# A sparse-attention, gated-MLP and token-mixing block on one core: v's tail between its pairs, the bias split in attention 0, merged x evictions, and batch 1's softmax with the main chain's priority

## The chip, the cores and the metric

The kernel runs on one core of one Trainium2 chip. The metric is the device time of one execution in microseconds (us). Runs are compared by their medians, and one execution of each kernel was recorded by the hardware profiler.

## The reference, cut to what matters

```
attn: q, k, v of 4 batches x 8 heads x 576 x 64
  heads 0-3: mask (0 <= i-j < 32);  heads 4-7: mask (i >= j and i%32 == j%32)
  x = softmax(mask(q k^T / 8)) v                    -> 4 x 576 x 512
h = relu(x @ w_in);  u, v = h[..., :512], h[..., 512:]
v_n = (v - mean(v)) / sqrt(var(v) + 1e-6)           over the 512 columns
x2 = (u * (w_spatial @ v_n + b_spatial)) @ w_out
theta = x2 @ w_theta
y = x2 + w_tok_r @ (x2 cos theta) + w_tok_i @ (x2 sin theta)
out = y + relu(y @ w_ch)
```

## The kernel before, in words

Every large product is made of float16 halves: an operand is split into a high and a low part, and three passes (high x high, low x high, high x low) go through TensorE. `PASS` is that list. The main chain of one batch is `main_v` (the v half of the first product, and its normalisation into `vn`), `main_mid` (u, the spatial product `sp`, the out product `x`, the theta product `th`) and `main_end` (the token product `y` and the channel product `c`). In `main_v` the 576 rows are two pairs of 128-row blocks (v0 and v1, one PSUM tile of two banks each) and a tail of 64 rows (v2). `v_relu` evicts a pair and takes the statistics of each block on VectorE; `norm` makes the reciprocal deviations of the blocks that it is given with `rstd`, 12 small VectorE operations on the tile `rs` whatever the number of columns, and `norm_q` then scales each block and splits it into high and low part.

Attention is a side chain. Batch 0's is `attention0`: nine groups of 64-row blocks in a software pipeline, s = 0 to 11, with scores, shift by the maximum (`gr_shift`, VectorE), exponential (`gr_exp`, ScalarE), transpose (`gr_turn`), product with v (`gr_pv`) and eviction into the two halves of `xT` (`gr_out`, which calls `gr_parts`). Within attention 0 each engine's instructions stay in the order in which the program gives them (the set `pinned`); the conversions of w_in are put between the steps by the table `aside`. After it, a list scheduler orders each engine's queue by priority and readiness. An operation called through `hv`, `ha` or `hg` has a priority 200 places ahead of its place in the program, and the main chain's vector and scalar operations use these; the attention of batches 1 and 2 (`attention1`, eight quads of blocks, with `qd_softmax` and `qd_div`) uses the plain priority. `others` puts the steps of attention and of the weight conversions (`conv`) between the main chain's matmuls by a count of matmul columns.

Three buffers of two PSUM banks (`pm`) serve the main chain's tiles and the attention's scores; two single banks (`sc` and `av`) serve attention's transposes and products. `gr_parts` evicts a PSUM bank in runs: blocks of one head that follow each other form a run, and each run costs one ScalarE and one VectorE operation, which take turns on the bank.

The bias of the spatial product, `b_sp`, stands with the tail of w_spatial in the tile `wspt`: row 64 holds its high part and row 96 its low part. `sp_tail` loads it on the SP queue into the staging buffer `x2f`, after the tail, and splits it there.

Of the kernel before, what the change touches and what calls it, by code (L numbers as in the profile page):

```python
# [19 lines left out]
ALU = mybir.AluOpType  # L20
# [12 lines left out]
AHEAD = 200  # L33
N32 = 3
LAG16 = 3
V_ORDER = (0, 1, 2)
E_WAY = 'aaaadaaadaa'
E_WHI = 'aaaa'
E_WLO = 'ggvv'
# [30 lines left out]
def kernel(  # L70
# [249 lines left out]
    def sp_tail():  # L320
        stg = pair(stage()[0].bitcast(F32), S)
        for j in range(2):
            nc.sync.dma_start(stg[j * TL:(j + 1) * TL, 0, :], w_spT[T0:S, :])
        nc.sync.dma_start(stg[TL:TL + 1, 1, :], b_sp)
        nc.sync.dma_start(stg[96:97, 1, :], b_sp)
        nc.scalar.activation(wspt[:, 0, :], stg[:, 0, :], AF.Copy, scale=SPS)
        nc.vector.scalar_tensor_tensor(wspt[0:TL, 1, :], stg[0:TL, 0, :], SPS, wspt[0:TL, 0, :],
                                       op0=ALU.mult, op1=ALU.subtract)
        nc.scalar.activation(wspt[TL:TL + 1, 1, :], stg[TL:TL + 1, 1, :], AF.Copy, scale=SPS)
        nc.scalar.activation(wspt[96:97, 1, :], stg[96:97, 1, :], AF.Copy, scale=SPS)  # L330
        nc.vector.scalar_tensor_tensor(wspt[96:97, 1, :], stg[96:97, 1, :], SPS, wspt[96:97, 1, :],
                                       op0=ALU.mult, op1=ALU.subtract)

    def tok_load(i, raw):
# [294 lines left out]
    def gr_parts(b, local, blocks, xt, by=1):  # L629

        xh = xT[b % 2]
        runs = []
        for i, (hp, blk) in enumerate(blocks):
            if runs and runs[-1][0] == hp and (local or blk < 10):
                runs[-1][3] += 1
            else:
                runs.append([hp, blk, i, 1])
        for hp, blk, i, n in runs:
            src = xt[:, QB * i:QB * (i + n)]
            if local:  # L640
                dst = [xh[:, e, hp, QB * blk:QB * (blk + n)] for e in range(2)]
            else:
                nr = min(3, STRIDE - 3 * blk)
                r0, o = (3 * (blk - blk % by), blk % by) if nr == 3 else (3 * blk, 0)
                dst = [xh[:, e, hp, :].rearrange("p (j r) -> p j r", r=STRIDE)
                       [:, :, r0:r0 + n * nr * (by if nr == 3 else 1)]
                       .rearrange("p j (n t r) -> p j n t r", n=n, r=nr)[:, :, :, o] for e in range(2)]
                src = src.rearrange("p (n c) -> p n c", c=QB)[:, :, 0:nr * NCLS].rearrange(
                    "p n (r j) -> p j n r", j=NCLS)
            nc.scalar.activation(dst[0], src, AF.Copy)  # L650
            nc.vector.tensor_tensor(dst[1], src, dst[0], ALU.subtract)

    def attention0(aside):

        xf = xT[1].rearrange("p e c n -> p (e c n)").bitcast(F32)
        vf = wtok.rearrange("p e i n -> p (e i n)").bitcast(F32)
        qk = kts + [xf[:, i * 2 * S:(i + 1) * 2 * S].rearrange("p (j n) -> p j n", j=2) for i in range(2)]
        q, k = [t[:, 0] for t in qk], [t[:, 1] for t in qk]  # L660
        v = [vf[:, i * 9 * VW:(i + 1) * 9 * VW].rearrange("p (n d) -> p n d", n=9) for i in range(2)]
        v23 = vf[:, 18 * VW:30 * VW].rearrange("p (h n d) -> p h n d", h=2, n=6)
        v += [v23[:, i] for i in range(2)]
        load_qk(0, 0, q[0], k[0], 0, 4 * QB)
        load_qk(0, 1, q[1], k[1], 0, S, nc.scalar)
        nc.scalar.activation(x2f[:, 0, 0:1], halfpi, AF.Exp)
        make_masks()
        load_qk(0, 0, q[0], k[0], 4 * QB, S)
        load_vl(0, 0, v[0])
        load_vl(0, 1, v[1])  # L670
        aside[-1][0]()
        load_qk(0, 2, q[2], k[2], 0, S)
        load_qk(0, 3, q[3], k[3], 0, S)
        aside[-1][1]()
        load_vs(0, v23)
        load_mask16()
        un = {}
        for s in range(NG + 3):
            mid, end = aside.get(s, ((), ()))
            if s < NG:  # L680
                if s % 4 == 3:
                    banks = pa("sc"), pa("av")
                else:
                    two = pm("at")
                    banks = two[:, 0, :], two[:, 1, :]
                t = s2("smx")
                sm, pT = t[:, 0, 0:384], t[:, 1, 0:512].rearrange("p (n k) -> p n k", n=4)
                st = att_p.tile([P, 2, 6], F32, tag="st", name="st", bufs=4)
                un[s] = banks, sm, pT, st
                gr_scores(s, q, k, banks[0])  # L690
                gr_shift(s, banks[0], sm, st)
            if s >= 3:
                banks, sm, pT, st = un.pop(s - 3)
                gr_out(0, s - 3, pT, banks[1])
            if 1 <= s <= NG:
                banks, sm, pT, st = un[s - 1]
                gr_turn(s - 1, sm, banks[1].rearrange("p (n k) -> p n k", n=4), pT)
            if s < NG:
                gr_exp(s, un[s][1])
            for f in mid:  # L700
                f()
            if 2 <= s < NG + 2:
                banks, sm, pT, st = un[s - 2]
                gr_pv(s - 2, v, pT, banks[0][:, 0:3 * VW].rearrange("p (i n) -> p i n", i=3), st, pT)
            for f in end:
                f()
# [42 lines left out]
        if not partial:  # L749
            masks()  # L750

    def qd_softmax(g, sc, sm, st):
        local, slots, ns, w = qd_size(g)
        n = 2 * ns
        sv = sc[:, :, 0:ns * w].rearrange("p j (n c) -> p j n c", c=w)
        mx = st[:, 0, 0:n].rearrange("p (j n) -> p j n", j=2)
        nc.vector.tensor_reduce(out=mx, in_=sv, op=ALU.max, axis=mybir.AxisListType.X)
        nc.vector.tensor_tensor(sm[:, 0:n * w].rearrange("p (j n c) -> p j n c", j=2, c=w), sv,
                                mx.unsqueeze(3).broadcast_to([P, 2, ns, w]), ALU.subtract)
        nc.scalar.activation(sm[:, 0:n * w], sm[:, 0:n * w], AF.Exp, scale=0.125)  # L760

    def qd_div(g, sm, st):

        local, slots, ns, w = qd_size(g)
        n = 2 * ns
        p, sums = sm[:, 0:n * w].rearrange("p (n c) -> p n c", c=w), st[:, 1, 0:n]
        nc.vector.tensor_reduce(out=sums, in_=p, op=ALU.add, axis=mybir.AxisListType.X)
        nc.vector.tensor_scalar(sums, sums, 1e-9, 1.0 / XS, op0=ALU.add, op1=ALU.mult)
        nc.vector.reciprocal(sums, sums)
        nc.vector.tensor_tensor(p, p, sums.unsqueeze(2).broadcast_to([P, n, w]), ALU.mult)  # L770

    def qd_places(g):

# [43 lines left out]
    def attention1(b):  # L817
# [20 lines left out]
        for s in range(NQ + 2):  # L838
            def turn():
                sm, pT, st = un[s - 1]  # L840
                qd_turn(s - 1, sm, pa4("av"), pT)

            if s == NQ:
                turn()
            if s >= 2:
                sm, pT, st = un.pop(s - 2)
                qd_px(b, s - 2, v, pT)
            if s < NQ:
                sm = att_p.tile([P, 512], F32, tag="sm", name="sm", bufs=2)
                pT = att_p.tile([P, 4, P], F32, tag="pT", name="pT32", bufs=2)  # L850
                st = att_p.tile([P, 2, 8], F32, tag="st", name="st", bufs=4)
                un[s] = (sm, pT, st)
                sc = pm("a1")
                qd_scores(s, q, k, sc)
                qd_softmax(s, sc, sm, st)
            if s in loads:
                f, hp = loads[s]
                f(hp)
            if 1 <= s < NQ:
                turn()  # L860
            if s < NQ:
                qd_div(s, *un[s][::2])
            yield


# [114 lines left out]
    def main_v(b):  # L980
# [43 lines left out]
        def v_mm(ps, i, c):  # L1024
            for n, (xe, we) in enumerate(PASS):
# [2 lines left out]
                    ps, xh[:, xe, c, i * P:(i + 1) * P], win[:, we, c, DM:2 * DM],  # L1028
                    start=(c == 0 and n == 0), stop=(c == NC - 1 and n == 2)).ins.name))

        if b == 0:
            ps = [pm("v0")]

# [11 lines left out]
            yield  # L1045
            some(1, (2,))
            yield
            for pr in range(2):
                some(pr, (3,))
                yield  # L1050
                v_relu(pr, ps[pr])
            norm((0, 1))
        for pr in V_ORDER if b else V_ORDER[2:]:
            ps = pm(f"v{pr}")
            if pr == 2:
                tail_mm(ps[:, 0, :], xh, win, slice(DM, 2 * DM))
                yield
            else:
                for t in range(2):
                    for c in range(NC):  # L1060
                        v_mm(ps[:, t, :], 2 * pr + t, c)
                    yield
            v_relu(pr, ps)
        norm((2,) if b == 0 else (0, 1, 2))

    def main_mid(b):
        xh = xT[b % 2]
# [332 lines left out]
```

## Time and profile before

| | us |
|---|---|
| median of 3 runs | 491.31 |
| the runs | 491.95, 491.31, 489.02 |
| the profiled execution | 488.88 |
| its span, first to last instruction | 487.0 |
| TensorE busy in the span | 467.9 |
| VectorE busy | 300.2 |
| ScalarE busy | 268.6 |
| GpSimd busy | 72.4 |

The span is what the trace covers; the 1.9 us between it and the execution's time lie outside of it. A matmul's busy time is modelled, so TensorE's share is read with the list of its waits beside it.

### The profile page before, as it was taken

What the parts mean: (1) busy time and instruction counts of PE and PEld (TensorE: products, weight loads), DVE (VectorE), ACT (ScalarE), POOL (GpSimd) and SP (SyncE); (2) the same over time, 40 slices, a digit from 0 to 9 for tenths busy, and PEclk for the clock granted to TensorE, in tenths of its full rate; (3) what the DMA queues carried; (4) which work ended last, traced back from release to release, by engine and by line L of the source; (5) the groups of instructions that cost most, each with busy time, mean ns of one, the idle gap of its engine ahead of it and who ended that gap; (6) DMA issues with size and microseconds to landing.
All of it is one profiled execution on the core that took longest, in us unless ns stands there. A gap on an engine that the chain in (4) does not pass through costs nothing. (4 is left out here: it accounts for less than half of the span.)

```text
span 487.0 us, 10793 instructions
## 1 busy us (share of the span) xinstructions
PE 467.9 (96%) x4440; PEld 351.5 (72%) x4440; DVE 300.2 (62%) x652; ACT 268.6 (55%) x480; POOL 72.4 (15%) x68
## 2 busy tenths in 40 slices
PE   6889998899999999999999999999999999999996
PEld 5665666677577778777568777777567777777775
DVE  3766997955998546752787878762686121227412
ACT  2668878788954334455945667754942022149202
POOL 2043025120015100201005110111005200210320
PEclk8999999999999999999999999999999999999999
DMA  6989446558860155100381345330450020003502
GB/s 177 288 260 286 187 138 217 171 182 243 158 153 1 63 168 147 54 1 2 85 216 53 88 125 159 66 44 1 68 127 2 1 98 0 1 2 74 122 0 99
DMA packets 71820, 52.72 MB, mean 108 GB/s; under 512 B 50584, under 2 KB 59992, under 8 KB 71770
## 3 DMA queue, kind: packets, MB, share of 16 engines
q1 hardware_dynamic: 71466, 51.42, 38.5%
q8 instruction: 35, 0.57, 0.5%
q10 hardware_dynamic: 304, 0.61, 0.4%
q14 instruction: 15, 0.12, 0.1%
HBM read 35.36 MB, written 4.72 MB: 82 GB/s over the span
## 5 line engine op out<-in xcount | busy, mean ns | idle before, releaser
L107 PE MATMUL y<-wtok,zf 128*128 128x288 f16 x864 | 107.2, 286 | 0.0
L107 PEld LDWEIGHTS <-zf 128*128 128x128 f16 x864 | 84.1, 98 | 22.2 <-issue 1.2
L107 PE MATMUL sp<-wsp,vn 128*128 128x288 f16 x384 | 50.7, 286 | 1.2 <-ACT u L107 1.2
L107 PE MATMUL x<-zf,wout 128*128 128x288 f16 x384 | 49.6, 287 | 0.0
L107 PE MATMUL v<-win,xT 128*128 128x512 f16 (+1 forms) x240 | 48.7, 380 | 0.9 <-DVE xT L107 0.6
L107 PE MATMUL u<-xT,win 128*128 128x288 f16 x384 | 49.2, 286 | 0.0
L107 PEld LDWEIGHTS <-vn 128*128 128x128 f16 x416 | 40.3, 98 | 11.4 <-issue 1.4
L107 PE MATMUL th<-x2h,wth 128*128 128x288 f16 x384 | 47.9, 286 | 0.0
L107 POOL TENSOR_TENSOR x2h<-x2f,x2h 128x576 f16<-128x576 f32 x19 | 26.2, 1382 | 142.4 <-issue 66.1
L107 PE MATMUL c<-x2h,wch 128*128 128x288 f16 x360 | 45.2, 286 | 0.0
L107 PEld LDWEIGHTS <-wth 128*128 128x128 f16 x384 | 37.6, 98 | 9.7 <-issue 0.2
L107 PEld LDWEIGHTS <-wch 128*128 128x128 f16 x384 | 37.4, 98 | 9.2
L107 PEld LDWEIGHTS <-win 128*128 128x128 f16 x384 | 37.4, 98 | 9.1
L107 PEld LDWEIGHTS <-wout 128*128 128x128 f16 x384 | 36.7, 98 | 9.5
L107 PEld LDWEIGHTS <-xT 128*128 128x128 f16 (+1 forms) x240 | 21.1, 100 | 24.9 <-issue 2.2
L107 ACT ACTIVATE x2h<-x2f 128x576 f16<-128x576 f32 (+1 forms) x28 | 20.9, 747 | 24.8 <-DVE x2f L107 23.5
L107 ACT ACTIVATE o<-c 128x576 f32<-128x576 f32 x15 | 9.7, 644 | 34.9 <-PE c L107 34.7
L107 DVE TENSOR_TENSOR ta<-ta,x2f 128x1152 f32<-128x1152 f32 (+1 forms) x17 | 21.7, 1284 | 11.2 <-ACT ta L107 11.2
L107 DVE SCALAR_TENSOR_TENSOR x2f<-y,x2f 128x576 f32<-128x576 f32 x16 | 12.0, 752 | 25.4 <-PE y L107 25.3
L107 POOL TENSOR_TENSOR zf<-u,zf 128x576 f16<-128x576 f32 x8 | 10.2, 1278 | 115.3 <-ACT zf L107 115.3
L107 DVE SCALAR_TENSOR_TENSOR o<-x2f,o 128x576 f32<-128x576 f32 (+1 forms) x17 | 12.2, 722 | 23.6 <-ACT o L107 23.6
L107 DVE TENSOR_TENSOR u<-u,sp 128x576 f32<-128x576 f32 x16 | 12.0, 750 | 22.2 <-PE sp L107 22.2
(144 smaller groups left out, 724.4 us busy)
## 6 DMA issues: line engine op xcount, KB each, us to landing
out_dram<-o SPq DMA_DIRECT2D x15, 288.0 KB
kt<-in_qp_dram SPq DMA_DIRECT2D x8, 288.0 KB
qs<-in_qd_dram SPq DMA_DIRECT2D x8, 288.0 KB
x2f<-in_w_in_dram SPq DMA_DIRECT2D x2, 1024.0 KB
zf<-in_w_in_dram SPq DMA_DIRECT2D x2, 1024.0 KB
xT<-in_w_ch_dram SPq DMA_DIRECT2D x2, 1024.0 KB
kt<-in_kzl_dram SPq DMA_DIRECT2D x8, 152.0 KB
ks<-in_kl_dram SPq DMA_DIRECT2D x4, 304.0 KB
```

The source lines that it names most:

```text
L107: ins = f(*args, **kwargs)
```

## The change

- **v's tail.** In batch 0 the tail's product and its eviction come after the first pair's last matmuls and before the second pair's, not after both. One `norm` over all five blocks takes the place of two (pairs, then tail). In the other batches the order stays.
- **Bias.** The two rows of the bias are loaded by two DMAs of GpSimd's queue into a tile of their own, behind the making of the masks, and split at the head of step s = 1 of attention 0: two ScalarE copies and a VectorE operation.
- **Merged evictions.** Where two neighbouring heads have the same single block in a bank, `gr_parts` evicts both in one run: one run fewer for the group that holds block 8 of heads 0 and 1, one fewer for the pair of last blocks in attention 0's group 6, and three fewer in the mixed quad of batches 1 and 2.
- **Priority.** `qd_softmax` and `qd_div` of batch 1 issue their VectorE operations through `hv`.

```diff
-        nc.sync.dma_start(stg[TL:TL + 1, 1, :], b_sp)
-        nc.sync.dma_start(stg[96:97, 1, :], b_sp)
...
-        nc.scalar.activation(wspt[TL:TL + 1, 1, :], stg[TL:TL + 1, 1, :], AF.Copy, scale=SPS)
-        nc.scalar.activation(wspt[96:97, 1, :], stg[96:97, 1, :], AF.Copy, scale=SPS)
-        nc.vector.scalar_tensor_tensor(wspt[96:97, 1, :], stg[96:97, 1, :], SPS, wspt[96:97, 1, :],
+
+    def bias_load():
+        t = s1("bias")
+        for r in (TL, 96):
+            nc.gpsimd.dma_start(t[r:r + 1, :], b_sp)
+        return t
+
+    def bias_part(t):
+        for r in (TL, 96):
+            nc.scalar.activation(wspt[r:r + 1, 1, :], t[r:r + 1, :], AF.Copy, scale=SPS)
+        nc.vector.scalar_tensor_tensor(wspt[96:97, 1, :], t[96:97, :], SPS, wspt[96:97, 1, :],
                                        op0=ALU.mult, op1=ALU.subtract)
...
-            if runs and runs[-1][0] == hp and (local or blk < 10):
+            if runs and runs[-1][0] == hp and runs[-1][4] == 1 and (local or blk < 10):
                 runs[-1][3] += 1
+            elif runs and runs[-1][0] == hp - 1 and runs[-1][1] == blk and runs[-1][3] == 1:
+                runs[-1][4] = 2
...
         make_masks()
+        bias = bias_load()
...
             mid, end = aside.get(s, ((), ()))
+            if s == 1:
+                bias_part(bias)
...
-    def qd_softmax(g, sc, sm, st):
+    def qd_softmax(b, g, sc, sm, st):
+        dv = hv if b == 1 else nc.vector
...
-        nc.vector.tensor_reduce(out=mx, in_=sv, op=ALU.max, axis=mybir.AxisListType.X)
+        dv.tensor_reduce(out=mx, in_=sv, op=ALU.max, axis=mybir.AxisListType.X)
...
-    def qd_div(g, sm, st):
+    def qd_div(b, g, sm, st):
+        dv = hv if b == 1 else nc.vector
...
+        def tail():
+            ps = pm("v2")
+            tail_mm(ps[:, 0, :], xh, win, slice(DM, 2 * DM))
+            yield
+            v_relu(2, ps)
...
+            some(0, (3,))
+            yield
+            v_relu(0, ps[0])
+            for _ in tail():
+                yield
+            some(1, (3,))
+            yield
+            v_relu(1, ps[1])
...
-        norm((2,) if b == 0 else (0, 1, 2))
+        norm((0, 1, 2))
```

## Rows read from the trace of the kernel before

**Rows 1.** What TensorE waited for, 31 to 106 us: total, times, longest.
```profile
PE av L107 <- DVE sm L107: 2.2, 4, 1.1
PE av L107 <- DVE xT L107: 1.7, 1, 1.7
PE sp L107 <- ACT u L107: 1.2, 1, 1.2
...
PE v L107 <- POOL win L107: 0.3, 1, 0.3
```
**Rows 2.** Busy time of each engine by stretch, granted clock, DMA share, GB/s.
```profile
48.47:61.51 13.04, 11.52 (x124) 8.69 (x123) 12.98 (x49) 10.82 (x17) 0.00 (x0) 1.00 0.51 189
61.51:89.64 28.13, 26.10 (x355) 19.48 (x355) 25.36 (x47) 22.01 (x33) 11.88 (x9) 1.00 0.55 180
89.64:107.69 18.05, 15.77 (x163) 11.78 (x161) 12.66 (x28) 14.27 (x25) 2.73 (x2) 1.00 0.59 192
...
119.62:487.00 367.38, 361.63 (x3220) 274.44 (x3217) 210.37 (x441) 181.58 (x346) 44.27 (x31) 1.00 0.30 74
```
**Rows 3.** TensorE in order of time: start, duration, instruction, idle before and releaser.
```profile
61.51 1.63 PE L107 MATMUL sp<-wsp,vn 128*128 128x288 f16 x12 [1.25 <-ACT u L107]
...
78.53 0.61 PE L107 MATMUL av<-ident,sm 128*96 128x128 f32 x4 [1.08 <-DVE sm L107]
...
93.55 0.65 PE L107 MATMUL av<-ident,sm 128*128 128x128 f32 x4 [1.67 <-DVE xT L107]
```
**Rows 4.** ScalarE in order of time, attention 0.
```profile
9.23 0.52 ACT L107 ACTIVATE smx<-smx 128x384 f32<-128x384 f32 x1 [5.33 <-DVE smx L107]
...
11.42 0.51 ACT L107 ACTIVATE smx<-smx 128x384 f32<-128x384 f32 x1
...
21.86 0.22 ACT L107 ACTIVATE xT<-at 128x64 f16<-128x64 f32 x1 [1.21 <-DVE xT L107]
```
**Rows 5.** The operations on the tile wspt: ns min/median/max, first and last start.
```profile
L107 ACT ACTIVATE wspt<-x2f x3: 666/679/679, 50.8 to 52.9; 1x576 f16<-1x576 f32 x2, 128x576 f16<-128x576 f32 x1
L107 DVE SCALAR_TENSOR_TENSOR wspt<-x2f,wspt x2: 736/746/755, 53.6 to 54.5; 64x576 f16<-64x576 f32 x1, 1x576 f16<-1x576 f32 x1
```
**Rows 6.** VectorE in order of time, step s = 1 of attention 0.
```profile
9.70 0.56 DVE L107 TENSOR_REDUCE st<-at 128x4 f32<-128x384 f32 x1 [0.51 <-PE at L107]
```
**Rows 7.** GpSimd in order of time: the last operation of the masks.
```profile
3.78 0.15 POOL L107 MEMSET mk<- 128x64 f32 x1
```
**Rows 8.** SP's queue in order of time: an early load of k.
```profile
1.20 1.44 SPq L107 DMA_DIRECT2D kt<-in_kzl_dram  x2
```
**Rows 9.** TensorE in order of time, attention 0.
```profile
6.86 0.87 PE L107 MATMUL at<-kt 64*64 64x96 f32 x14 [0.66 <-DMA kt<-in_kzl_dram]
...
22.40 0.34 PE L107 MATMUL at<-mask,identb 128*128 128x384 bf16 x1 [0.91 <-DVE xT L107]
```
**Rows 10.** VectorE in order of time, main chain and batch 1.
```profile
55.92 0.42 DVE L107 TENSOR_TENSOR rs<-rs 128x4 f32<-128x4 f32 x4
...
62.54 0.55 DVE L107 TENSOR_TENSOR sm<-sm,st 128x384 f32<-128x384 f32 x1
...
76.61 0.74 DVE L107 TENSOR_TENSOR u<-u,sp 128x576 f32<-128x576 f32 x1
...
77.67 0.71 DVE L107 TENSOR_TENSOR sm<-sm,st 128x384 f32<-128x384 f32 x1
...
93.10 0.40 DVE L107 TENSOR_TENSOR xT<-av,xT 128x216 f16<-128x216 f32 x1
```
**Rows 11.** ScalarE in order of time, v's eviction and batch 1.
```profile
45.31 2.11 ACT L107 ACTIVATE vr<-v 128x1024 f32<-128x1024 f32 x2 [0.33 <-PE v L107]
...
82.98 1.29 ACT L107 ACTIVATE zf<-zf 128x1152 f32<-128x1152 f32 x1 [0.77 <-DMA zf<-in_w_tr_dram]
...
90.09 1.17 ACT L107 ACTIVATE wtok<-wx 128x1152 f16<-128x1152 f32 x1 [0.67 <-DVE wx L107]
```
**Rows 12.** Busy time by stretch where TensorE's granted clock was low.
```profile
8.50:9.00 0.50, 0.50 (x10) 0.44 (x6) 0.47 (x2) 0.00 (x0) 0.00 (x0) 0.50 0.66 194
```

More of the change, by code (lines that the diff above doesn't have):

```diff
@@ L35 @@
 LAG16 = 3
-V_ORDER = (0, 1, 2)
 E_WAY = 'aaaadaaadaa'
@@ L633, in gr_parts @@
         for i, (hp, blk) in enumerate(blocks):
-            if runs and runs[-1][0] == hp and (local or blk < 10):
+            if runs and runs[-1][0] == hp and runs[-1][4] == 1 and (local or blk < 10):
                 runs[-1][3] += 1
-            else:
[L637 to L640, printed above, removed]
+            elif runs and runs[-1][0] == hp - 1 and runs[-1][1] == blk and runs[-1][3] == 1:
+                runs[-1][4] = 2
+            else:
+                runs.append([hp, blk, i, 1, 1])
+        for hp, blk, i, n, heads in runs:
+            src = xt[:, QB * i:QB * (i + n * heads)]
+            if heads == 2:
+                src = src.rearrange("p (h c) -> p h c", h=2)
+                dst = [xh[:, e, hp:hp + 2, :] for e in range(2)]
+                if local:
+                    dst = [d[:, :, QB * blk:QB * (blk + 1)] for d in dst]
+                else:
+                    nr = min(3, STRIDE - 3 * blk)
+                    dst = [d.rearrange("p h (j r) -> p h j r", r=STRIDE)[:, :, :, 3 * blk:3 * blk + nr] for d in dst]
+                    src = src[:, :, 0:nr * NCLS].rearrange("p h (r j) -> p h j r", j=NCLS)
+            elif local:
                 dst = [xh[:, e, hp, QB * blk:QB * (blk + n)] for e in range(2)]
@@ L756, in qd_softmax @@
         mx = st[:, 0, 0:n].rearrange("p (j n) -> p j n", j=2)
-        nc.vector.tensor_reduce(out=mx, in_=sv, op=ALU.max, axis=mybir.AxisListType.X)
-        nc.vector.tensor_tensor(sm[:, 0:n * w].rearrange("p (j n c) -> p j n c", j=2, c=w), sv,
+        dv.tensor_reduce(out=mx, in_=sv, op=ALU.max, axis=mybir.AxisListType.X)
+        dv.tensor_tensor(sm[:, 0:n * w].rearrange("p (j n c) -> p j n c", j=2, c=w), sv,
                                 mx.unsqueeze(3).broadcast_to([P, 2, ns, w]), ALU.subtract)
         nc.scalar.activation(sm[:, 0:n * w], sm[:, 0:n * w], AF.Exp, scale=0.125)
-    def qd_div(g, sm, st):
+    def qd_div(b, g, sm, st):
+        dv = hv if b == 1 else nc.vector
         local, slots, ns, w = qd_size(g)
@@ L766, in qd_div @@
         p, sums = sm[:, 0:n * w].rearrange("p (n c) -> p n c", c=w), st[:, 1, 0:n]
[L767 to L770, printed above, removed]
+        dv.tensor_reduce(out=sums, in_=p, op=ALU.add, axis=mybir.AxisListType.X)
+        dv.tensor_scalar(sums, sums, 1e-9, 1.0 / XS, op0=ALU.add, op1=ALU.mult)
+        dv.reciprocal(sums, sums)
+        dv.tensor_tensor(p, p, sums.unsqueeze(2).broadcast_to([P, n, w]), ALU.mult)
     def qd_places(g):
@@ L854, in attention1 @@
                 qd_scores(s, q, k, sc)
-                qd_softmax(s, sc, sm, st)
+                qd_softmax(b, s, sc, sm, st)
             if s in loads:
@@ L861, in attention1 @@
             if s < NQ:
-                qd_div(s, *un[s][::2])
+                qd_div(b, s, *un[s][::2])
             yield
@@ L1047, in main_v @@
             yield
-            for pr in range(2):
[L1049 to L1058, printed above, removed]
+            some(0, (3,))
[6 more added lines that the diff above has]
+            v_relu(1, ps[1])
+        else:
+            for pr in range(2):
+                ps = pm(f"v{pr}")
                 for t in range(2):
@@ L1062, in main_v @@
                     yield
-            v_relu(pr, ps)
-        norm((2,) if b == 0 else (0, 1, 2))
+                v_relu(pr, ps)
+            for _ in tail():
+                yield
+        norm((0, 1, 2))
     def main_mid(b):
```

## The prediction

> **What bounds the kernel now.** I read TensorE's waits first, then the busy time by stretch, then the order of time of each engine around the waits. TensorE is busy nearly all of the span, so only its waits can be won; the change takes no matmul away. Behind 119.62 us there is little: 361.63 of 367.38 us are busy [rows 2], and the only edit that reaches there is batch 2's merged evictions. Between 31 and 106 us the waits that matter are 2.2 us for batch 1's softmax on VectorE, 1.7 us for one eviction into xT, 1.2 us for a u eviction and 0.3 us for a part of w_in [rows 1]. In that time VectorE is the tight engine: 12.98 of 13.04 us busy while v is normalised, 25.36 of 28.13 us while sp runs, 12.66 of 18.05 us in x [rows 2]. So an operation taken from VectorE's queue, or put further up in it, moves what TensorE waits for; and everything put ahead pushes something else back. Attention 0 is different: each engine keeps program order there, and the chain back from the first v matmul runs through VectorE and ScalarE without slack to step 1's exponential at 11.42 us [rows 4]: TensorE's products hang on it, then step 3's exponential, and behind that on ScalarE the conversions of w_in.
>
> **Part by part.**
>
> *Bias in attention 0.* Step 1 gets two ScalarE copies of 0.67 us and a VectorE operation of 0.75 us [rows 5], ahead of its own work. ScalarE ends the first exponential at 9.75 us [rows 4]. If the two rows have landed by then, the copies end at about 11.0 us; the transposed tile that ScalarE evicts next is ready at about 10.9 us, so ScalarE loses 0.1 us at most. VectorE loses more: its operation needs the second copy, and queued behind it are the two operations of the step's shift, the first from 9.70 us [rows 6], the second as long and right behind it. They now start at about 11.0 + 0.75 = 11.75 us and end 0.56 + 0.56 us later, at 12.9 us. The exponential that waits for them moves from 11.42 to 12.9 us: 1.4 us on the chain, which I carry to v's first matmul. The bounds are 0 (something later in attention 0 hides all of it; an added operation ahead in a queue can't win) and 1.4 us plus a wait for the data, below. I take 1.4, since I see no slack between 11.42 and 31 us.
>
> *When the bias lands.* No GpSimd DMA is in the trace. The masks end on GpSimd at 3.9 us [rows 7], and the nearest row is an early load of k: issued on SP's queue from 1.20 to 2.64 us, waited for by TensorE until 6.86 us [rows 8, 9], so 4.2 us from the end of the issue to use. With the two issues taking nothing the bias is there at 8.1 us, 1.6 us early; with 1.4 us for each of the two issues (what SP needs for its pair) it is there at 10.9 us, 1.2 us late. I take no wait, nearer to the first end, because two single rows are small beside that load. The rest of GpSimd's queue behind the issues is four short fills of v's ones, which no product reads before step 2.
>
> The Trainium skill speaks against this queue: "SBUF — State Buffer", section "SBUF: two separate sides", says that a GpSimd DMA has its descriptors written by GpSimd, and that some VectorE operations lock it out of the port meanwhile. Six VectorE casts of the masks stand just there; by an estimate from "DMA: Bandwidth & Descriptors" (about 2 us fixed for each) the rows would land between 7 and 10 us, and the sum would gain a wait of at most 0.3 us. No row of this trace shows such a transfer.
>
> *Merged evictions.* At step 5 of attention 0 the second head's ScalarE copy waits 1.21 us for VectorE [rows 4], and TensorE's next scores wait 0.91 us for the bank until VectorE's second part is done [rows 9]. One run of both heads ends about 0.45 us sooner (one 0.22 us copy and one part less), and the steps behind it follow: -0.45 us. At group 6 the same saves a wait of 0.2 us. The wait of 0.3 us for w_in [rows 1] hangs on GpSimd and the DMAs, not on attention, and is covered by the delay. So v's last matmul comes 1.4 - 0.45 - 0.2 - 0.3 = about 0.5 us later than before. In batches 1 and 2 three ScalarE and three VectorE operations of some 0.2 us fall away each in the mixed quad; I count -0.2 us for batch 1 and nothing for batch 2.
>
> *Norm in one piece.* VectorE loses 12 small operations of about 0.1 us (four take 0.42 us [rows 10]), 11 of them ahead of the point at which the first vn parts are ready, and the bias operation of 0.75 us: 1.85 us of a queue that is full in this stretch [rows 2]. ScalarE loses 1.3 us there. Against it: v ends 0.5 us later, and batch 1's pending operations now pass the normalisation; the last one that stood behind it, 0.55 us at 62.54 us [rows 10], may come ahead: +0.5 us. So the chain ends 0.85 us sooner.
>
> *The tail between the pairs.* The tail needs the third PSUM buffer of its kind, and v0, v1 and batch 1's first scores hold all three. It is free when v0's eviction ends: 45.31 us plus half of 2.11 us [rows 11]. If TensorE's queue has the tail straight behind v0's last matmul it waits about 0.9 us; if the scheduler lets v1's last six matmuls pass, nothing is lost and nothing is gained, except that the one norm now waits for the tail's statistics, with other VectorE work to fill the time. 0 to 0.9 us; a gain is excluded, since the matmuls are the same. I take 0.35: the wait would fall ahead of a stretch whose end VectorE sets, not TensorE. Start of sp: 61.51 [rows 3] - 0.85 + 0.35 = -0.5 us. More than the 1.25 us wait there can't be won.
>
> *Priority.* Of the 2.2 us that TensorE waits for batch 1's softmax, 1.9 us fall behind 61.51 us, the largest at 78.53 us [rows 1, 3]. There the division ends at 78.3 us because a main-chain product of 0.74 us went ahead of it [rows 10]; with the same priority the attention step was issued first and goes first. I take all 1.9 us. The product it passes comes at most 0.7 us later, under 3 us of sp matmuls. Bounds: 0 to -2.2.
>
> *What is late next.* At 93.55 us TensorE waits 1.67 us for bank av [rows 3]. Its eviction ends on VectorE at 93.5 us [rows 10], because on ScalarE it stands behind a part of w_tok that waits for VectorE until 90.09 us [rows 11]. Evictions and conversions keep the plain priority, so batch 1's softmax now passes them too. If that gate stays, all that was won before it is lost (+2.4 us); if it moves along, nothing is. The data would let it move: the transfer behind that part had landed at 82.98 us [rows 11], and three conversions of about 1.3 us each end at 87, 3 us ahead of 90.09. I take a quarter of the loss, +0.6 us.
>
> **Sum.** -0.5 (start of sp) - 1.9 (softmax) + 0.6 (the gate) - 0.2 (merges) = -2.0 us. On the profiled execution that is 488.88 - 2.0 = 486.9 us. That execution lies 2.4 us under the median of the runs, so I forecast for the median 491.31 - 2.0 = 489.3 us.
>
> **The rivals.**
> - *Given back at 93.55 us.* The 2.4 us won before it only lengthen that wait. For it: the gate hangs on operations of low priority on a full VectorE. Against it: the 3 us of room. Of the sum only -0.2 us stays: 491.1 us.
> - *Slower: the bias lands late.* ScalarE and VectorE stand still at the heads of their queues from 9.75 us on; each microsecond is one on the chain. It decides from a landing at 11.8 us, 2 us late, where the whole gain is gone. At 8.50 us TensorE runs at its lower level of 1.2 GHz (granted 0.50 [rows 12]), after it had stood idle for k until 6.86 us [rows 9]; a pause of 2 us and more just behind that can keep or bring back this level. Another 3.5 us at it would do what full clock does in 1.75 us; I count 1 us of the loss as on the path. 2 + 1 us: 492.3 us. For it: nothing shows this queue's speed. Against it: two transfers of 2.3 KB.
> - *The tail isn't moved.* The buffers are full, v1's matmuls pass, and the norm waits for the tail as well: 0.5 us lost instead of won, so 490.3 us.
> - *Nearly all waits go.* The 1.25 us at sp, 1.9 us of softmax and half of the 1.67 us, with attention 0 hiding the bias: -4.0 us, 487.3 us.
>
> On the clock in the slower rival, the Trainium skill ("TensorE: Matmul & The Clock Gate", "HAM oscillation — how this bites in real kernels") says that waits on data set TensorE back to half clock again and again; the row at 8.50 us agrees for one such wait, and whether the new pause brings another no row can show.
>
> **How the numbers follow.** Forecast 0.44, given back 0.22, tail not moved 0.10, nearly all 0.13, slower 0.11. The three runs before lie 2.9 us apart, so a median of three carries some 1 us on top. The range goes from 486.0 (nearly all, less 1.3) to 492.6 us (the slower rival and a little). 1% of this kernel, 4.9 us, is about what a measurement tells from no change. Faster by more than that needs 486.4 us, half of the best rival's tail: 0.07. Slower by more needs 496.2 us, a bias 5 us later still: 0.03. Within: 0.90.
>
> **What the profile after would show.** Right: the exponential of step 1 at about 12.9 us, v's first matmul about 0.9 us later than 31.4, one set of 12 operations on rs, sp at about 61.0 us, no wait of TensorE for sm above 0.3 us before 90 us, a wait of 1.5 to 2.5 us for bank av in x, and two xT operations on 128 columns where four on 64 stood. Wrong: ScalarE waiting for the bias at 9.75 us; a wait of v for a buffer near 45 us; a longer wait for vn at sp, because batch 1 passed the normalisation; or a different order behind 119.62 us, which the scheduler may choose for reasons that I can't read from this trace.

## The result and the profile after

| | before | after |
|---|---|---|
| median (11 runs each) | 490.3 | 493.45 |
| the runs | 488.85 to 491.95 | 491.35 to 495.3 |
| the profiled execution | 488.88 | 495.3 |
| its span | 487.0 | 493.5 |

The changed kernel is slower: ratio 1.006 with a 95% interval of 1.0038 to 1.0081, 3.15 us by the medians. The forecast was 489.3 us and the range ended at 492.6. Its base, a median of three, was 1.0 us above the median of eleven; the forecast change was -2.0 us, the measured one +3.15. The profiled execution of before is one of its fastest and that of after its slowest, so 3.3 us of the 6.4 us between them belong to the executions and not to the kernels, and the profiled executions of e9 and e17 below (803.5 and 500.2 us, beside 495.8 to 497.0 and 489.5 to 494.3 of their others) are left out of the times and not read.

TensorE's waits after (of [rows 1] the same view; total, times, longest), 31 to 115 us:

```profile
PE av L106 <- DVE sm L106: 3.1, 2, 2.5
PE av L106 <- ACT zf L106: 2.3, 1, 2.3
PE v L106 <- DVE xT L106: 1.3, 1, 1.3
```

Busy time by stretch after (columns as in [rows 2]): v's end to sp, sp, x; then two short stretches of sp.

```profile
51.85:68.47 16.62, 13.51 (x162) 10.34 (x163) 16.42 (x47) 13.48 (x20) 3.20 (x3) 0.99 0.50 166
68.47:98.29 29.82, 27.17 (x333) 20.26 (x333) 26.03 (x41) 23.18 (x33) 10.67 (x8) 0.89 0.48 158
98.29:113.97 15.68, 15.39 (x162) 11.58 (x160) 9.17 (x20) 8.91 (x17) 0.00 (x0) 1.00 0.61 188
...
68.00:71.50 3.50, 3.39 (x15) 2.17 (x16) 3.47 (x4) 3.50 (x6) 0.44 (x1) 0.53 0.03 14
92.00:95.00 3.00, 3.00 (x16) 1.92 (x14) 3.00 (x4) 3.00 (x4) 0.72 (x1) 0.52 0.24 65
```

From theta's product on (107.69 before, 113.97 after) both spans take 379.3 and 379.5 us, so 6.3 of the 6.5 us between the spans stand ahead of it: the first v matmul is 4.8 us later (31.39 and 36.19), v itself 0.8 us shorter, from its end to sp it takes 16.62 us where it took 13.64 (47.87 to 61.51), sp is 1.7 us longer, x 2.4 us shorter. TensorE ran at its lower level (granted 0.53 and 0.52) in two stretches of sp where before had none.

The timeline after: ScalarE, VectorE and TensorE in step 1 of attention 0 (for before see [rows 4] and [rows 6]), v's first matmul and its last weight loads, VectorE and GpSimd while v is normalised, and TensorE in sp:

```profile
10.28 0.52 ACT L106 ACTIVATE smx<-smx 128x384 f32<-128x384 f32 x1 [6.40 <-DVE smx L106]
10.83 1.38 ACT L106 ACTIVATE wspt<-bias 1x576 f16<-1x576 f32 x2
...
14.21 0.52 ACT L106 ACTIVATE smx<-smx 128x384 f32<-128x384 f32 x1 [1.39 <-DVE smx L106]
...
12.24 0.76 DVE L106 SCALAR_TENSOR_TENSOR wspt<-bias,wspt 1x576 f16<-1x576 f32 x1 [1.99 <-ACT wspt L106]
13.03 0.56 DVE L106 TENSOR_REDUCE st<-at 128x4 f32<-128x384 f32 x1
...
14.79 1.09 PE L106 MATMUL at<-ident,smx 128*96 128x128 f32 x4 [1.74 <-ACT smx L106]
...
36.19 1.45 PE L106 MATMUL v<-win,xT 128*128 128x512 f16 x6 [1.28 <-DVE xT L106]
...
50.26 1.11 PEld L106 LDWEIGHTS <-xT 128*64 128x64 f16 x12 [0.42 <-issue]
...
55.35 0.68 DVE L106 BATCH_NORM_STATS2 bs<-vr 64x6 f32<-64x512 f32 x1
...
57.14 1.27 DVE L106 BATCH_NORM_STATS2 bs<-vr 128x6 f32<-128x512 f32 x2
...
59.05 0.17 DVE L106 TENSOR_SCALAR rs<-mv 128x5 f32<-128x5 f32 x1
...
62.10 1.34 DVE L106 TENSOR_TENSOR rs<-rs 128x5 f32<-128x5 f32 x2
63.48 1.09 DVE L106 SCALAR_TENSOR_TENSOR rs<-rs 128x5 f32<-128x5 f32 x1
...
64.95 0.16 DVE L106 TENSOR_TENSOR rs<-rs 128x5 f32<-128x5 f32 x1
...
62.26 2.28 POOL L106 TENSOR_TENSOR wout<-x2h,wout 128x512 f16<-128x512 f32 x2 [11.18 <-ACT wout L106]
...
68.11 0.57 PE L106 MATMUL av<-ident,sm 128*96 128x128 f32 x2 [2.48 <-DVE sm L106]
...
83.95 3.10 PE L106 MATMUL sp<-wsp,vn 128*128 128x288 f16 x24
...
91.39 0.63 PE L106 MATMUL av<-ident,sm 128*128 128x128 f32 x4 [2.27 <-ACT zf L106]
91.86 4.65 PE L106 MATMUL sp<-wsp,vn 128*128 128x288 f16 x23
```

The rows of before beside them:

```profile
31.39 1.24 PE L107 MATMUL v<-win,xT 128*128 128x512 f16 x5 [0.56 <-DVE xT L107]
...
46.28 1.10 PEld L107 LDWEIGHTS <-xT 128*64 128x64 f16 x12 [0.42 <-issue]
...
48.32 1.27 DVE L107 BATCH_NORM_STATS2 bs<-vr 128x6 f32<-128x512 f32 x2
...
50.77 0.15 DVE L107 TENSOR_SCALAR rs<-mv 128x4 f32<-128x4 f32 x1
...
50.94 0.69 DVE L107 BATCH_NORM_STATS2 bs<-vr 64x6 f32<-64x512 f32 x1
```

Four things are to be seen. The bias had landed: ScalarE starts on it right behind the exponential, without a wait. VectorE stands 1.99 us for the second copy with the shift queued behind it, and the exponentials lie 3.93 us apart where they lay 2.19 apart [rows 4]. The tail's twelve weight loads (64 columns) come last of v, as before: TensorE's order in v didn't change, but on VectorE the tail's statistics (55.35) now stand ahead of v1's (57.14), where v1's came first (48.32 and 50.94), and the rs chain starts at 59.05, 7.2 us behind v's end, where it started 2.9 us behind it (50.77 and 47.87). And each of the two stretches at the lower level follows a wait of over 2 us; 23 sp matmuls take 4.65 us there and 24 take 3.10 us elsewhere.

### The profile page after: what moved, and what is told of

It is laid out like the page before. It is cut to its first block, busy times and chain, and to the rows that moved or that the text cites. A ratio compares the mean times of both kernels' runs of the same rounds, so it can differ in the third digit from the quotient of the medians.

```text
span 493.5 us, 10770 instructions
## 1 busy us (share of the span) xinstructions
PE 473.0 (96%) x4440; PEld 356.2 (72%) x4440; DVE 301.9 (61%) x630; ACT 267.7 (54%) x470; POOL 72.7 (15%) x70
## 5 line engine op out<-in xcount | busy, mean ns | idle before, releaser
L106 PE MATMUL sp<-wsp,vn 128*128 128x288 f16 x384 | 52.2, 293 | 0.0
L106 PE MATMUL u<-xT,win 128*128 128x288 f16 x384 | 50.2, 290 | 0.0
L106 PEld LDWEIGHTS <-vn 128*128 128x128 f16 x416 | 41.5, 100 | 11.2 <-ACT vn L106 0.2
```

The source lines that it names most:

```text
L106: ins = f(*args, **kwargs)
```

## The experiments

In the end two theories were set against each other (e13 to e16): **own cost** (each part costs what it adds, the bias split above all) and **other order** (the list scheduler makes another order of everything behind attention 0 as soon as anything is moved, and that order is worse). The runs ahead of them name theories of their own, each explained in the expectation that it first stands in. Times are medians of five to twelve executions (e9: three), before on the same chip beside them.

| run | median | before | ratio (95%) |
|---|---|---|---|
| e1 bias alone | 493.73 | 490.54 | 1.0065 (1.004 to 1.009) |
| e2 tail and one norm alone | 496.54 | 490.54 | 1.0121 (1.0079 to 1.0163) |
| e3 priority alone | 492.86 | 490.54 | 1.004 (1.001 to 1.0071) |
| e4 merged evictions alone | 488.92 | 490.54 | 0.996 (0.9937 to 0.9984) |
| e5 all but tail and norm | 493.41 | 489.52 | 1.0075 (1.0055 to 1.0095) |
| e6 all but bias | 493.65 | 489.52 | 1.0079 (1.0065 to 1.0094) |
| e7 one norm, old order of v | 491.68 | 489.52 | 1.0047 (1.0034 to 1.0059) |
| e8 new order of v, two norms | 489.88 | 489.52 | 1.0018 (1.0 to 1.0037) |
| e9 all but priority | 496.86 | 490.06 | 1.0134 (1.0118 to 1.0149) |
| e10 bias loaded early, split moved back in the program | 492.96 | 490.06 | 1.0066 (1.0042 to 1.009) |
| e11 priority from quad 3 on | 494.15 | 490.06 | 1.0085 (1.0063 to 1.0106) |
| e12 e10 and merged evictions | 491.85 | 490.06 | 1.0028 (1.0003 to 1.0053) |
| e13 bias early, added, order kept | 493.52 | 489.56 | 1.0078 (1.0062 to 1.0095) |
| e14 before, attention start 3.0 | 489.92 | 489.56 | 1.0012 (0.9997 to 1.0028) |
| e15 before, attention gap 4.3 | 491.39 | 489.56 | 1.0038 (1.0024 to 1.0052) |
| e16 changed kernel, gap 4.3 | 494.14 | 489.56 | 1.0085 (1.007 to 1.0099) |
| e17 e13 with the loads alone | 491.83 | 489.72 | 1.0026 (1.0003 to 1.0049) |
| e18 e13, VectorE's part two places later | 490.66 | 489.72 | 1.002 (1.0001 to 1.0038) |

**One part at a time (e1 to e4).** Each has its own hunks of the diff above and nothing else: e1 `bias_load` and `bias_part`, e2 `tail` and `norm((0, 1, 2))`, e3 the `dv` lines, e4 `gr_parts`.

> The kernel before with the bias edit alone. Theory B (the two copies and the VectorE operation at the head of step 1 hold up attention 0's chain, and the pause keeps TensorE at its lower level): 1.5 to 3.5 us slower than before, the step-1 exponential some 1.4 us or more later, v's first matmul 2 to 4 us later. Theory N (the loss is made in the normalisation of v) and theory P (batch 1's priority): -0.5 to +0.5 us, what attention 0 loses is hidden by VectorE's backlog in v's stretch.

> The kernel before with v's tail between the pairs and one norm, nothing else. Theory N (one norm begins only when the statistics of v1 and the tail are done, and its small operations then meet GpSimd's part of w_out): 1 to 3 us slower, the first operation on rs about 4 us behind where it was against v's end, sp later. Theory B: 0 to 1 us faster, by 12 small VectorE operations fewer. Theory P: within 0.5 us.

> The kernel before with batch 1's softmax through hv, nothing else. The prediction's step: 1.5 to 2 us faster, with no wait of TensorE for sm over 0.3 us. Theory P (batch 1's operations pass the normalisation and the u products, so the main chain pays): 0.5 to 2 us slower, sp begins later. Theories B and N say nothing against the gain here: 0.5 to 2 us faster.

> The kernel before with the merged evictions alone. All theories: 0.3 to 1 us faster, v's first matmul 0.3 to 0.6 us earlier, since four operations fewer stand in attention 0's chain. If it is slower, the new order that the scheduler finds behind attention 0 is a cause of its own, and theories B, N and P aren't all.

Measured: +3.2, +6.0, +2.3 and -1.6 us. e1 came as theory B said; e2 lost more than any theory allowed, e3 slightly more than theory P, and e4 won more than the 1 us of all of them. Three of four lose, the sum (+9.9) is three times the whole change's loss, and e4 is faster than both kernels. At step 5 its merged copy shows what was forecast (timeline, ScalarE, e4):

```profile
18.93 0.52 ACT L107 ACTIVATE smx<-smx 128x384 f32<-128x384 f32 x1
21.17 0.28 ACT L107 ACTIVATE xT<-at 128x128 f16<-128x128 f32 x1 [1.72 <-PE at L107]
21.61 0.59 ACT L107 ACTIVATE smx<-at 96x512 f32<-96x512 f32 x1 [0.16 <-PE at L107]
22.16 0.52 ACT L107 ACTIVATE smx<-smx 128x384 f32<-128x384 f32 x1
```

The exponentials of steps 4 and 5 are 3.23 us apart; before, they were 3.64 apart (18.82 and 22.46): 0.4 us won, 0.45 forecast.

**All but one (e5, e6, e9).** The lines are shortened.

```diff
 e5:  some(pr, (3,)); v_relu(pr, ps[pr]); norm((0, 1)); ... norm((2,) if b == 0 else (0, 1, 2))
 e6:  b_sp loaded and split in sp_tail, as before
 e9:  dv = nc.vector
```

> The changed kernel without v's new order and the single norm (bias, merged evictions and priority stay). Theory S (the new order costs what it cost alone, about 6 us): 3 us faster than the kernel before and 6 us faster than the changed one. Theory A (the parts lose the same time in v's normalisation, so they don't add up; with the other parts there the new order costs little): 0 to 4 us slower than the kernel before, like the changed one.

> The changed kernel with the bias back in the tail's load of w_spatial. Theory B (1.4 us and more of attention 0's chain comes through to the end): 2 to 4 us faster than the changed kernel, within 1 us of the kernel before. Theory A: less than 1 us from the changed kernel, because attention 0's delay is hidden by the longer normalisation behind it.

> The changed kernel with batch 1's softmax back at plain priority. Additive theory: 2.3 us faster than the changed kernel, as the priority alone cost the kernel before that much. Clock theory (the loss is made of TensorE waits of 1.5 us and more between 60 and 100 us, each followed by a stretch at 1.2 GHz that costs some 1.5 us more; which edit makes the wait matters little): within 1.5 us of the changed kernel, with one or two such stretches in the rows behind 32 us; if its trace has none, it is 2.5 to 4 us faster than the changed kernel.

Measured: +3.9, +4.1 and +6.8 us. e5 and e6 came as theory A said, e9 as neither of its two. None of these three parts can be taken out and the loss with it (the change without the merges was not run): without the bias it is as large, without the priority it is twice as large. So the priority wins some 3.7 us inside the whole change and loses 2.3 us alone.

**Which half of a part (e7, e8, e10, e11, e12).** The lines are shortened.

```diff
 e7:   -norm((0, 1))   -norm((2,) if b == 0 else (0, 1, 2))   +norm((0, 1, 2))
 e8:   tail() between some(0, (3,)) and some(1, (3,)), the two norms of before
 e10:  bias = bias_load() behind make_masks(); bias_part(bias) in sp_tail
 e11:  dv = hv if b == 1 and g >= 3 else nc.vector
 e12:  e10 with gr_parts of the change
```

> The kernel before with one norm over all five blocks, in the old order (pairs, then tail). Theory one-norm (the reciprocal deviations have to wait for the tail's statistics, and that is what the new order pays for): 3 to 6 us slower. Theory order (v1's eviction and statistics come behind the tail's, since the tail itself can't move on TensorE): -1 to +1.5 us, 12 small VectorE operations fewer against 1 to 2 us of waiting.

> The kernel before with the new order of the tail, and two norms as before (pairs, then tail). Theory order: 3 to 6 us slower, v1's statistics on VectorE behind the tail's and some 5 us later against v's end than before. Theory one-norm: -1 to +1 us.

> The kernel before with the bias loaded early by GpSimd, but split in the old place, with the tail of w_spatial. Queue theory (the operations at the head of step 1 cost, not the load): within 1 us of the kernel before, step 1's exponential 1.7 to 2.2 us behind step 0's instead of 3.9, no late v. Load theory (GpSimd's DMA or the memory traffic disturbs attention 0): 2 to 3.5 us slower, as with the whole edit.

> The kernel before with the main chain's priority for batch 1's softmax from quad 3 on alone, so that quads 0 to 2, which stand beside v's normalisation, keep the plain one. Theory P (the first quads pass the normalisation and so make long waits at sp): 1 to 3 us faster than with the priority for all quads, so -1 to +1 us against the kernel before, and no stretch at 1.2 GHz near 72 us. Rival (the later quads push the conversions of weights back): 1.5 to 3 us slower than the kernel before, as with all quads.

> Merged evictions and the bias loaded early but split in the old place, nothing else: the parts that should pay. Queue theory: 1 to 2.5 us faster than the kernel before, as with the merged evictions alone (1.6 us), or some tenths better. Load theory: 0.5 to 2 us slower.

Measured: +2.2, +0.4, +2.9, +4.1 and +1.8 us. e7 lies between its two theories, e8 came as the one-norm theory said, e10 and e12 as the load theory, e11 lost more than its rival. One norm alone measures 2.2 us, though it takes away 12 VectorE operations: all five blocks wait for the slowest statistics, so that in e7's profile the rs chain starts 5.5 us behind v's end (54.75 and 49.27) and sp 1.7 us later behind it than before. The new order of v with two norms costs nothing that is clear. e10 was read as clearing the split: early or late, the edit lost 3 us. That was the ground for the theory of the other order, and the next runs were made to try it.

The traces don't bear that reading of e10, and they show a rival for several of these losses. The lines of e10, then of e2, ScalarE, VectorE and TensorE:

```profile
7.83 1.38 ACT L107 ACTIVATE wspt<-bias 1x576 f16<-1x576 f32 x2 [3.93 <-DMA bias<-in_b_sp_dram]
...
12.04 0.76 DVE L107 SCALAR_TENSOR_TENSOR wspt<-bias,wspt 1x576 f16<-1x576 f32 x1
...
18.33 1.15 ACT L107 ACTIVATE x2f<-x2f 128x1024 f32<-128x1024 f32 x1 [1.30 <-DMA x2f<-in_w_in_dram]
```

```profile
18.05 1.12 ACT L106 ACTIVATE x2f<-x2f 128x1024 f32<-128x1024 f32 x1 [1.71 <-DMA x2f<-in_w_in_dram]
...
20.95 0.32 PE L106 MATMUL at<-mask,identb 128*128 128x384 bf16 x1 [2.58 <-DVE xT L106]
```

The split of e10, and of e12, was not late: the schedule has all three operations in attention 0, VectorE's right behind step 1's shift, where the exponentials are not held up (10.13 and 12.33, 2.20 us apart). So neither run tried a late split. And in the profiles of e2, e6, e7, e10, e11 and e12 ScalarE waits 0.8 to 1.7 us in attention 0 for a part of w_in, which it doesn't in before's; TensorE then stands 1.7 to 2.6 us, runs at its lower level right behind that, and starts v 1.8 to 5.0 us later than in before's profile. e2, e6, e7 and e11 change nothing ahead of that wait, so this share of their loss is not the edit's own work in the profile; whether the other executions have it too is not recorded.

**Work with the order kept, order with the work kept (e13 to e16).** In e13 every other instruction keeps its place on every engine (the lines are shortened).

```diff
 e13, to the kernel before (old loads and split stay):
+        bias = bias_load()          # behind make_masks()
+            if s == 1:
+                bias_part(bias)
 e14: -ATT_AT = (None, (2.7, 4.2), ...   +ATT_AT = (None, (3.0, 4.2), ...
 e15: -ATT_AT = (None, (2.7, 4.2), ...   +ATT_AT = (None, (2.7, 4.3), ...
 e16: the line of e15 in the changed kernel
```

> The kernel before, with the two early loads of the bias on GpSimd and its split at the head of step 1 of attention 0 put in as an addition: the old loads and the old split stay too, so that all other instructions keep the order of before on every engine. It measures what the moved operations cost at their new place, without any other order behind them. Theory own cost (what the bias edit lost, +3.2 us alone, is the 1.7 us in attention 0 and what follows from it): +2.0 to +3.5 us against before, TensorE's first v matmul 1.5 us later or more, theta's first product as much later. Theory other order (the loss comes from the order that the scheduler makes behind attention 0): 0 to +1.2 us, the waits of the kernel before at sp and x, and no stretch at 1.2 GHz between 60 and 116 us.

> The kernel before with one number of its schedule changed: the steps of batch 1's attention begin at 3.0 instead of 2.7 thousand matmul columns. No instruction is added or taken away; 100 rows of TensorE's queue, 14 of VectorE's and 18 of ScalarE's stand at other places. Theory own cost (parts of the change cost what they add): -0.7 to +0.7 us. Theory other order (the order before is a well fitted one, and any other makes new waits and a stretch at 1.2 GHz): +1.0 to +4.0 us, with a wait of TensorE over 1.5 us between 60 and 116 us that the kernel before does not have.

> As the run before it, with the other number: batch 1's steps are 4.3 instead of 4.2 thousand columns apart. 176 rows of TensorE's queue, 86 of VectorE's and 70 of ScalarE's stand at other places, no work changes. Theory own cost: -0.7 to +0.7 us. Theory other order: +1.0 to +4.0 us, with stretches of TensorE at 1.2 GHz between 60 and 116 us.

> The whole change with the same number changed (4.3 instead of 4.2 thousand columns between batch 1's steps): the work of the changed kernel in another order, with 180 rows of TensorE's queue at other places. Theory own cost: within 0.8 us of the changed kernel, so +2.3 to +3.9 us against before. Theory other order: it may come out anywhere from -2 to +6 us against before, and moves with the number of stretches at 1.2 GHz between 60 and 116 us: none gives 489 to 490.5 us, two give 493 to 494 us, three give 496 us.

Measured: +4.0, +0.4, +1.8 and +4.6 us. e13 settles the bias: the theory of the other order allowed +1.2 us at most and falls for this part. The delay is made in attention 0 and is only handed on: v's first matmul comes 4.6 us later than before, its end 4.1, theta's first product 3.5 (111.21 and 107.69), the end of the span 3.9; 0.7 us of it stands already at the first exponential, ahead of the split (9.92 and 9.23). It is half a microsecond more than the own cost allowed. Another order alone costs 0.4 us in e14, not clear of zero and as the own cost said, and 1.8 us in e15, as the other order said. e16 moved 180 rows of TensorE's queue and lost 4.6 us, no less than the changed kernel and more than the own cost allowed.

**Which instruction (e17, e18).**

```diff
 e17, to e13:
-            if s == 1:
-                bias_part(bias)
 e18, to e13 (bias_part without its VectorE operation; bias_low is that operation):
             for f in end:
                 f()
+            if s == 1:
+                bias_low(bias)
```

> The kernel before with only the two early loads of the bias on GpSimd added, into a tile that nothing reads; the old loads and the old split stay, and every other instruction keeps its place. The run with early loads and early split added lost 3.96 us. Theory split (what costs is the split at the head of step 1, where VectorE stands 2.0 us and the exponential 1.7 us): -0.7 to +0.7 us here, gap between the first two exponentials 1.8 to 2.2 us. Theory load (GpSimd's two transfers, 1.14 us of its queue, hold up what lands in attention 0, w_in above all): +2.0 to +4.0 us, with ScalarE's or VectorE's work on w_in waiting for a DMA by 1 us or more.

> As the run with early loads and early split added, but with one instruction two places later in VectorE's queue: its part of the split comes behind the two shift operations of step 1 instead of ahead of them. ScalarE's two copies stay at the head of the step. Theory head wait (the loss is VectorE standing for the second copy with the shift queued behind): -0.5 to +1.0 us, gap between the first two exponentials 1.8 to 2.6 us, no wait of TensorE for the exponential above 1 us and less than 4 us at 1.2 GHz ahead of 32 us. Theory work (any 2.1 us of operations put into attention 0 cost what they take): +2.0 to +3.5 us, gap 3 us or more.

Measured: +2.1 us (by the ratio +1.3, interval 0.15 to 2.4) and +0.9 us (0.05 to 1.9). e17 decides between neither of its theories; e18 came as the head wait said, but for a wait of TensorE of 1.08 us. Moving one VectorE instruction of 0.76 us two places back gives back 3 of the 4 us. The loads alone can't be told from e18, which has them too. The timelines of e13 and then e18, VectorE, ScalarE and TensorE:

```profile
11.88 0.76 DVE L107 SCALAR_TENSOR_TENSOR wspt<-bias,wspt 1x576 f16<-1x576 f32 x1 [2.00 <-ACT wspt L107]
...
13.85 0.52 ACT L107 ACTIVATE smx<-smx 128x384 f32<-128x384 f32 x1 [1.39 <-DVE smx L107]
...
14.43 1.09 PE L107 MATMUL at<-ident,smx 128*96 128x128 f32 x4 [2.63 <-ACT smx L107]
...
16.56 1.55 PE L107 MATMUL sc<-kt 64*64 64x96 f32 x16
```

```profile
11.17 0.56 DVE L107 TENSOR_TENSOR smx<-at,st 128x384 f32<-128x384 f32 x1
11.82 0.76 DVE L107 SCALAR_TENSOR_TENSOR wspt<-bias,wspt 1x576 f16<-1x576 f32 x1
...
12.43 0.52 ACT L107 ACTIVATE smx<-smx 128x384 f32<-128x384 f32 x1
...
13.00 0.64 PE L107 MATMUL at<-ident,smx 128*96 128x128 f32 x4 [1.08 <-ACT smx L107]
...
14.24 0.88 PE L107 MATMUL sc<-kt 64*64 64x96 f32 x16
```

Behind the shift the same operation starts at the same time (11.82 and 11.88) and nothing in attention 0 waits for it. The stretch behind it by windows, e13 (with the next one) and e18:

```profile
14.40:17.90 3.50, 3.47 (x36) 2.89 (x36) 0.84 (x4) 0.84 (x2) 0.00 (x0) 0.50 1.03 333
17.90:21.50 3.60, 3.60 (x43) 2.85 (x40) 2.21 (x6) 2.45 (x5) 0.00 (x0) 0.61 1.05 312
```

```profile
14.40:17.90 3.50, 3.17 (x55) 2.46 (x54) 2.88 (x9) 2.07 (x5) 0.00 (x0) 1.00 1.03 351
```

Behind its wait of 2.63 us TensorE runs e13's stretch at 1.2 GHz (granted 0.50): 36 matmuls are done where e18 does 55, and VectorE and ScalarE starve behind it. From the first to the fourth exponential e13 takes 9.85 us (9.92 to 19.77), e18 6.76 (9.85 to 16.61), before 6.36 (9.23 to 15.59) and after 9.84 (10.28 to 20.12). So the 3.5 us lost there are 1.74 us by which the second exponential is late and as much again behind it. The granted clock is 0.50 in this stretch and 0.61 in the next, which is enough to account for the second half; e18, whose first half is missing, hasn't the second either.

## Why the prediction was wrong

**Bias in attention 0: the step that failed in the clearest test.** "The exponential that waits for them moves from 11.42 to 12.9 us: 1.4 us on the chain" had the right mechanism, and its sign in the profile came (14.21, or 1.74 us by the gap). The bounds "0 and 1.4 us plus a wait for the data" were wrong: the term measured 4.0 us (e13). What it left out is that TensorE stands still for that exponential, and that a stretch at 1.2 GHz follows. The prediction had this chain, but only in the rival of a late bias, with 1 us counted on the path; the bias was not late, and the chain came all the same. Nor was it asked whether the operation had to stand there: e18 shows that it didn't. This step is not the whole loss: the change without it (e6) lost 4.1 us.

**When the bias lands.** Right: no wait at 10.83 us. In e10, where ScalarE waits for the rows, they are there at 7.83 us, slightly ahead of the early end of the forecast (8.1). The Trainium skill's rule against GpSimd's queue ("SBUF — State Buffer", section "SBUF: two separate sides") did not bite; the two issues took 1.14 us and the rows were there.

**Tail and norm.** "-0.5 us at the start of sp" failed. The rival "the tail isn't moved" was true for TensorE, and worse than its 0.5 us: in the profile sp starts 3.0 us later behind v's end than before, because the chain on rs starts 4.3 us later. e7 puts 2.2 us on the one norm, e8 0.4 us on the order. Together (e2) they measured 6.0 us; of the 3.4 us more, the wait for w_in shown above is a rival that no run excludes. "With other VectorE work to fill the time" was the mistake: VectorE is full in that stretch, so that other work was not filler, it was queued ahead of v1's statistics.

**Priority.** "I take all 1.9 us" failed, though the waits that were named went: from 78.07 to 88 us no wait for sm is left, and the gate at 93.55 moved along (0.3 us are left of its 1.67, x is 2.4 us shorter). But the order that carries it has new ones, 2.48 us for sm at 68.11 and 2.27 us at 91.39, which the profile puts down to a zf operation of ScalarE, and the sign "no wait for sm above 0.3 us" is wrong. At 91.39 the softmax was late on the other engine: its shift ended at 86.59, but its exponential, on ScalarE and not moved by the edit, started at 88.23, behind a weight conversion. Alone the priority loses (e3: +2.3 us), beside the other parts it wins (3.7 us).

**Merges.** Right in place and mechanism: 0.85 us forecast in three terms, 1.6 us measured in e4 (0.8 to 3.1 us by the interval), 0.4 us of it seen at step 5. In e12 beside e10 they are worth 1.1 us by the medians.

**What no term had.** The sum took the waits of before as given and edited them one by one. The scheduler made another order of what lies behind attention 0; e15 shows that this alone can cost 1.8 us here without any change of work (e14: 0.4 us, not clear of zero). And no term had the clock behind v. The record gives a mean granted clock for every execution: its median is 0.990 after, and 0.997 to 1.000 in the rounds of before beside the experiments. By an estimate from these, the missing share of the clock times the span, that is 4.9 us after and 1.5 us or less before, so 3.4 us or more between them, about the whole 3.15 us. The runs that lose most have the lowest clock (e9 0.982, e2 0.986), e4 and e18 have 0.999. It is an estimate and not a test: a reading can be 1.00 where matmuls run at half rate (after, 14.40 to 17.90, where four into at take 1.09 us and e18's take 0.64), and e15 loses 1.8 us at 0.999.

**What stays open.** The parts don't add: +9.9 us singly, +3.1 together, and +4.1 without the bias, although the bias alone costs 4. So the delay of the bias and the losses behind v must overlap in the whole change; which wait covers which was not tried, and which step made its 3.15 us stays open. The 2.9 us of e10, whose operations stand much as in e18, are not explained either: in its profile the first v matmul is 3.0 us later than before's, behind the wait for w_in, and whether the early loads hold up w_in is open, since e2 and e7 have the same wait without them and e18 has them without the wait.

## What to carry to other kernels

Where an engine's queue is in program order, the place of an added instruction can count for more than its duration (e13 and e18: 4.0 and 0.9 us): put it behind the operations that something waits for, above all when it needs another engine's result first. When a delay makes TensorE stand, price the stretch behind it at both clock levels. And test an edit with all other orders kept before blaming or praising the schedule: a run that adds the work and leaves the old in place (e13) told what no combination of the parts could. Look in the trace whether an edit put its instructions where it was meant to (e10's were not late), and don't place a loss by one profiled execution alone: v starts up to 5.0 us apart in kernels that are the same up to there (before and e2).

## What was not expected of the hardware

**Small VectorE operations beside a GpSimd operation.** After v, rs operations on 128x5 that elsewhere take 0.16 us took 1.34 us for two and 1.09 us for one, from 62.10 to 64.57 us, while GpSimd's two operations of 1.14 us ran from 62.26 to 64.54. The Trainium skill ("SBUF — State Buffer", section "SBUF: two separate sides") says that VectorE and GpSimd share a port pair, taken for a whole instruction, and that a VectorE operation with two SBUF inputs needs it against a GpSimd operation that reads SBUF; these rows agree.

**The same wait, two sequels.** In batch 1's x product TensorE waited 1.77 us in e15 for a matmul into av and then ran at granted 0.52; in e14 it waited 1.89 us for the same matmul, and the next 19 ran at full rate (timelines and a window of e15, then e14):

```profile
94.84 1.04 PE L107 MATMUL av<-ident,sm 128*128 128x128 f32 x4 [1.77 <-DVE xT L107]
95.67 3.58 PE L107 MATMUL x<-zf,wout 128*128 128x288 f16 x17
...
95.00:98.50 3.50, 3.50 (x17) 2.38 (x17) 2.46 (x4) 2.13 (x3) 0.84 (x1) 0.52 1.03 307
```

```profile
95.47 0.66 PE L107 MATMUL av<-ident,sm 128*128 128x128 f32 x4 [1.89 <-DVE xT L107]
95.97 2.49 PE L107 MATMUL x<-zf,wout 128*128 128x288 f16 x19
```

So in these rows the length of a wait alone doesn't tell whether the clock falls. Nor is that stretch what e15 lost: of its nine executions four have a mean granted clock of 1.000 and took 491.19 to 492.26 us, and the profiled one, with the stretch, has 0.997 and took 491.28.
